# Two pairs of heads share their last 64 keys in a quartered attention, with loads one pair further ahead

## The chip, the cores and the metric

The kernel runs on one core of a Trainium2 chip. The metric is the device time of one execution in microseconds; the kernel before takes 988.81 us (median of three runs, 988.07 to 988.83). Four engines matter here: TensorE (PE in the profile) multiplies matrices into PSUM, which has eight banks; VectorE (DVE) and ScalarE (ACT) work elementwise; SyncE (SP) issues the DMAs that bring data from HBM. Each engine takes its instructions in the order in which the program gives them, and waits where one of them needs a result that is not there.

## The reference

Three stages, all in float32, on 1792 tokens (4 batches of 448) and 768 features:

```
# attention: 4 batches, 12 heads, 448 positions, 64 wide, with a sigmoid in place of the softmax
attn = sigmoid(q @ k.T / sqrt(64) - log(448));  x = attn @ v          # heads joined: 1792 x 768
# gated layer
xn = x / sqrt(mean(x*x) + 1e-6) * g;  x2 = (silu(xn @ w_gate) * (xn @ w_val)) @ w_out   # 768 -> 1536 -> 768
# experts: each token to the one of 8 with the largest logit
e = argmax(x2 @ gate);  out = p_e * (relu(x2 @ w1[e]) @ w2[e])                          # 768 -> 1024 -> 768
```

The weights of the gated layer reach the kernel as 64-bit numbers, 128 x 768 at a time, and have to be made into 32-bit ones on the chip.

## The kernel before

The work goes batch by batch. `attention(b)` makes the 768 x 448 block of one batch; `moe1(b)` is the gated layer on it; the experts come after all four batches. The program is written out by hand in the order in which each engine is to take it: generators yield after each small step, and a driver takes steps of several of them in turn. Attention of batch b+1 is taken in steps between the pieces (nine matmuls each) of `moe1(b)`.

Batches 0 and 1 use `in_quarters`. It takes the heads in six pairs, and the 448 keys of a pair in four steps: three of 128 keys, and a last one of 64. A matmul there is 64 x 64 x 448 in float32, done in two passes (two instructions), and uses a quarter of the 128 x 128 array: which half of the rows it uses follows from the half of the partitions from which it reads, which half of the columns from the half into which it writes. `quarters(t)` makes the scores of a step: with 128 keys that is four quarters (two heads, two blocks of 64 keys), which fill the array. With the last 64 keys there are two, on one diagonal: head 0 on the upper rows and left columns, head 1 on the lower rows and right columns. `weights(t)` is ScalarE's sigmoid out of PSUM, one instruction for each bank: two in a full step, one in the last. `weighted(t)` multiplies by the values, again four quarters or two, and adds up in two banks, `sums`, one for each half of the rows:

```
sums[p][i][h], v4[o, c, x, :], a[x if c < NC - 1 else 0][o],       # L686
```

After the last step of a pair `both` (L693) adds the two banks: ScalarE copies one into `xt` (L695), VectorE adds the other (L696). Two steps later ScalarE squares the result (L600, L603), and VectorE adds the squares up (L604), for the root mean square. Weighted sums lag behind the scores by two steps in batch 0, by one in batch 1.

The scores of a step wait for PSUM banks: even steps use two `sc` banks, odd steps two `mm` banks, which the gated layer uses later.

Loads. `load_pair` (L503) brings q and k of a pair, `load_v` (L514) its values; the pair goes into one of two buffers (`RQK = 2`). At the first step of a pair the next pair is loaded, into the buffer that the pair before has just left; at its third step, the next pair's values. All of it is issued by SP, in the order of the program, between the loads of 64-bit weights, `load_64` (L203).

Conversion of the weights. `narrow` (L211) takes one 128 x 768 block of 64-bit words: three instructions of VectorE (L219, L223, L227), and then the load of the block three further on. There are 36 blocks. While attention of batch 0 runs, the driver takes one and two of these instructions in turn at the steps 2 to 21, which is 30 of them, 10 blocks:

```
for _ in range(1 + n % 2 if 2 <= n < 22 else 0):                  # L1198
    next(conv)
```

In `moe1(0)` five go with each unit of 36 matmuls (`operations_due`); `ahead` (L282) takes more where the next unit's block would be missing. `split_w` (L243) then makes of each block a high part (ScalarE, L250) and a low part (VectorE, L253) for the three matmuls of `three` (L297 to L299). The first two of these splits stand at the steps 20 and 22 of attention of batch 0.

The pace of attention of batch 1 inside `moe1(0)` is `attention_due` (L53): 26 steps, spread over 55 pieces. Six of its steps have been taken before, while batch 0's last sums go through the root mean square (L773 to L817).

Of the kernel before, what the change touches and what calls it, by code (L numbers as in the profile page):

```python
# [9 lines left out]
F32 = mybir.dt.float32  # L10
F32R = mybir.dt.float32r
# [8 lines left out]
B, H, S, D = 4, 12, 448, 64  # L20
# [9 lines left out]
NC = S // CT  # L30
# [16 lines left out]
RQK = 2  # L47

KW = S + 64


def attention_due(b, n):

    main = H // 2 * NC + 2 if b == 0 else H * NC + 5
    if n < 55:
        return main * (n + 1) / 55
    return main + n - 54
# [39 lines left out]
def f32(ap):  # L97
    return ap.bitcast(F32)
# [3 lines left out]
def block_kernel(ctx, tc, qkp, qk, v, wg, wv, wo, g, gate, w1, w2, consts, out):  # L102
    nc = tc.nc
# [13 lines left out]
    s_a, aq = opened("aq", side="right", reuse_waits="tile")  # L117
# [15 lines left out]
    start = cpool.tile([128, 1], F32, name="start")  # L133
# [111 lines left out]
    def split_w(n, i):  # L245
        w = w32.pop(2 * n + i)
        h = wp.tile([128, KD, 128], F32R, tag="wh", name="wh", bufs=3)
        l = wp.tile([128, KD, 128], F32R, tag="wl", name="wl", bufs=3)
        w3 = w.rearrange("p (c k) -> p c k", k=128)
        nc.scalar.copy(out=h, in_=w3)  # L250

        def low():
            nc.vector.tensor_tensor(out=l, in0=w3, in1=f32(h), op=ALU.subtract)  # L253
            split_done[0] += 1
            if NU <= n + 1 < NU * B:
                load_32(n + 1, i)

        later(1, low)
        spl[n, i] = (h, l)
# [243 lines left out]

    def load_pair(b, p):

        r = aq.tile([128, S + KW], F32, tag="rqk", name="rqk", bufs=RQK)
        nc.sync.dma_start(out=r[:, : 2 * S], in_=qkp[b, p])
        raw_a[b, "pair", p] = r

    raw_v = {}  # L510
# [1 line left out]
    gated = []  # L512

    def load_v(b, p):  # L514
        rv = aq.tile([128, 4 * 128], F32, tag="rv", name="rv", bufs=2)
# [24 lines left out]
    def attention(b):  # L540
# [89 lines left out]
        def in_quarters():  # L630

            sums, score, weight = {}, {}, {}
            mm = [m[:, :S] for m in spare]
            n = H // 2 * NC
            halves = [slice(0, D), slice(D, 2 * D)]

            def quarters(t):
                p, c = divmod(t, NC)  # L640
                r = raw_a[b, "pair", p]

                if c % 2 and not gated:
                    banks = mm[: 1 + (c < NC - 1)]
                else:
                    banks = [sc_bank([128, S], "psc") for x in range(1 + (c < NC - 1))]
                for x, h in enumerate(halves):
                    for i, o in enumerate(halves):
                        if c < NC - 1:
                            k = S + 128 * c + D * i  # L650
                            to = banks[x][o]
                        elif i == x:
                            k = S + 128 * c
                            to = banks[0][o]
                        else:
                            continue
                        nc.tensor.matmul(to, r[h, k : k + D], r[h, :S], start=True, stop=True)  # L657
                score[t] = banks

            def weights(t):  # L660
                act = dict(func=AF.Sigmoid, bias=logs, scale=1.0 / math.sqrt(D))
                weight[t] = []
                for i, p in enumerate(score.pop(t)):
                    if t % NC == NC - 1:
                        a = f32(aq.tile([128, S], F32R, tag="al", name="aj", bufs=3))
                    elif i == 0:
                        a = aq.tile([128, S], F32, tag="a", name="a", bufs=4)
                    else:
                        a = f32(aq.tile([128, S], F32R, tag="ah", name="a2", bufs=4))
                    nc.scalar.activation(out=a, in_=p, **act)  # L670
                    weight[t].append(a)

            def weighted(t):
                p, c = divmod(t, NC)
                if c == 0:
                    if b == 0 and p % 2:
                        sums[p] = [mm[2], mi_bank([128, S], "pav")]
                    else:
                        sums[p] = [av_bank([128, S], "pav") for i in range(2)]
                a = weight.pop(t)  # L680
                v4 = raw_v[b, p].rearrange("s (c j d) -> s c j d", j=2, d=D)
                for x, h in enumerate(halves):
                    for i, o in enumerate(halves):
                        if c == NC - 1 and i != x:
                            continue
                        nc.tensor.matmul(  # L686
                            sums[p][i][h], v4[o, c, x, :], a[x if c < NC - 1 else 0][o],
                            start=(c == 0), stop=(c == (NC - 1 if i == x else NC - 2)),
                        )
                if c == NC - 1:  # L690
# [12 lines left out]
            fresh()  # L703
            coming = iter(())
            lag = 2 - b
            for t in range(n + lag):
                p, c = divmod(t, NC)
                if t < n:
                    if c == 0 and p > 0:
                        load_next(p + 1)  # L710
                    if c == 2:
                        load_v(*((b, p + 1) if p + 1 < H // 2 else (b + 1, 0)))
                    quarters(t)
                if t == n:
                    load_next(H // 2 + 1)
                    if b == 1:
                        coming = prep(2, 0)
                if t >= lag:
                    weighted(t - lag)
                step()  # L720
                if t < n:
                    weights(t)
                next(coming, None)
                yield
            for _ in coming:
                pass

        def load_next(p):
            if p < H // 2:
                load_pair(b, p)  # L730
            elif b == 0:
                load_pair(1, p - H // 2)
            else:
                load_qk(2, p - H // 2)
# [447 lines left out]


    att = {b: attention(b) for b in range(B)}
    for n in range(H // 2 * NC + 2):
# [12 lines left out]
        for _ in range(1 + n % 2 if 2 <= n < 22 else 0):  # L1198
            next(conv)
        tick()  # L1200
        if n in (20, 22):
            split_w(0, n // 2 - 10)
    ahead_of = 0
    for _ in att[0]:
        tick()
# [202 lines left out]
```

## Time and profile before

| | |
|---|---|
| runs (us) | 988.83, 988.81, 988.07; median 988.81 |
| profiled execution | 988.29 us, of it 986.2 us from the first to the last instruction |
| granted TensorE clock, mean | 0.998 of full speed |
| busy, share of the span | PE 98%, PEld (weight loads) 84%, DVE 65%, ACT 47%, POOL 2% |
| chain that ended last | PE 85%, DVE 6%, DMA 4%, ACT 1% |
| quartered matmuls in it | L657 (scores) and L686 (values), batches 0 and 1 |

In the profile a step of quartered attention shows as rows of L657 and L686. A matmul's own time there is long, as it holds the way through the array; what one costs is read from the distance between starts. The first attention lies from 4 to 45 us, the root mean square after it up to 58 us, the gated layer of batch 0 with attention of batch 1 between its pieces from 58 to 247 us.

### The profile page before, as it was taken

The numbers are of one execution on the slowest core, as the hardware profiler recorded it, in microseconds if no ns is written. First come the engines' busy times: TensorE is split into PE (matmuls) and PEld (weight loads), VectorE is DVE, ScalarE is ACT, GpSimd is POOL, SyncE is SP. The second block draws the span as 40 slices with busy tenths as digits, with TensorE's granted clock in tenths as the row PEclk, the third lists the DMA queues.
The fourth block names the chain that finished last, engine by engine and source line by source line (L and its number), as shares of the span: only waits on it lengthen the run. The fifth ranks groups of instructions, "written<-read, shape, count | busy, mean of one in ns | idle before, by whom it ended". The sixth has DMA issues, their size and how long they took to land.

```text
span 986.2 us, 14474 instructions
## 1 busy us (share of the span) xinstructions
PE 963.8 (98%) x5334; PEld 829.0 (84%) x5334; DVE 637.2 (65%) x1103; ACT 463.6 (47%) x776; POOL 14.9 (2%) x43
## 2 busy tenths in 40 slices
PE   8989999989999999999999999999999999999996
PEld 3467766777999999899999988999889988889996
DVE  5778866787798774779877465654446744444454
ACT  6743443424788872578877233332322232232230
POOL 0000000020000001000000100000000000000000
PEclk9999999999999999999999999999999999999999
DMA  8949653677544435644342569433577659838632
GB/s 323 341 166 350 243 192 119 211 244 228 184 123 138 154 101 165 195 167 126 124 144 80 143 219 319 129 99 129 142 220 235 199 172 370 296 113 289 170 65 52
DMA packets 121457, 184.33 MB, mean 187 GB/s; under 512 B 62538, under 2 KB 79690, under 8 KB 121377
## 3 DMA queue, kind: packets, MB, share of 16 engines
q1 hardware_dynamic: 119344, 182.55, 57.3%
q8 instruction: 44, 0.72, 0.3%
q0 software_dynamic: 144, 0.53, 0.2%
q10 hardware_dynamic: 1888, 0.23, 0.2%
q14 instruction: 37, 0.30, 0.1%
HBM read 145.26 MB, written 37.88 MB: 186 GB/s over the span
## 4 chain that ended last, share of the span: by engine, by line
PE 85%; DVE 6%; DMA 4%; ACT 1%; issue 1%; SPq 1%; POOL 1%; DVEq 0%; ACTq 0%
PE mm L297 19%; PE mm L298 19%; PE mm L299 19%; PE sc L297 4%; PE sc L298 4%; PE sc L299 4%; PE pav L584 2%; PE psc L551 2%; PE psc L657 2%; PE psc L552 2%; PE pav L686 2%; PE pav L586 1%; DMA xd<-x2s 1%; DVE wl L253 1%; DVE xl L808 1%
## 5 line engine op out<-in xcount | busy, mean ns | idle before, releaser
L297 PE MATMUL mm<-xh,wh 128*128 128x448 f32 x576 | 213.5, 371 | 1.3 <-ACT xh L817 1.0
L298 PE MATMUL mm<-xl,wh 128*128 128x448 f32 x576 | 210.8, 366 | 0.2 <-DVE xl L808 0.2
L299 PE MATMUL mm<-xh,wl 128*128 128x448 f32 x576 | 210.1, 365 | 0.0
L253 DVE TENSOR_TENSOR wl<-w,wh 128x768 fp32r<-128x768 f32 x126 | 119.5, 948 | 30.8 <-ACT wh L250 26.4
L250 ACT CAST wh<-w 128x768 fp32r<-128x768 f32 x126 | 105.5, 838 | 52.7 <-PE mm L298 23.2
L297 PEld LDWEIGHTS mm<-xh,wh 128*128 128x128 f32 x576 | 108.2, 188 | 24.5 <-issue 9.6
L298 PEld LDWEIGHTS mm<-xl,wh 128*128 128x128 f32 x576 | 108.2, 188 | 8.8 <-DVE xl L808 0.5
L299 PEld LDWEIGHTS mm<-xh,wl 128*128 128x128 f32 x576 | 108.2, 188 | 8.7
L297 PE MATMUL mm<-hs,wh 128*128 128x448 f32 x288 | 106.3, 369 | 0.3 <-DVE xr L344 0.3
L299 PE MATMUL mm<-hs,wl 128*128 128x448 f32 x288 | 105.4, 366 | 0.1
L298 PE MATMUL mm<-hs,wh 128*128 128x448 f32 x288 | 105.5, 366 | 0.0
L297 PE MATMUL sc<-hh,w2h 128*128 128x448 f32 (+1 forms) x200 | 72.0, 360 | 0.5 <-DVE yt L910 0.5
L298 PE MATMUL sc<-hl,w2h 128*128 128x448 f32 (+1 forms) x200 | 71.2, 356 | 0.0
L299 PE MATMUL sc<-hh,w2l 128*128 128x448 f32 (+1 forms) x200 | 71.2, 356 | 0.0
L297 PE MATMUL mm<-xd,w1h 128*128 128x448 f32 x192 | 70.8, 369 | 0.0
L298 PE MATMUL mm<-xd,w1h 128*128 128x448 f32 x192 | 70.1, 365 | 0.0
L299 PE MATMUL mm<-xd,w1l 128*128 128x448 f32 x192 | 70.1, 365 | 0.0
L561 ACT ACTIVATE a<-psc,logs 128x448 f32<-128x448 f32 x96 | 61.4, 640 | 15.7 <-PE psc L552 12.0
L891 ACT ACTIVATE hh<-mm 128x448 fp32r<-128x448 f32 x32 | 17.4, 544 | 105.2 <-PE mm L299 105.2
L563 ACT ACTIVATE ah<-psc,logs 128x448 fp32r<-128x448 f32 x96 | 60.9, 635 | 0.0
L297 PEld LDWEIGHTS mm<-hs,wh 128*128 128x128 f32 x288 | 54.1, 188 | 7.9 <-issue 1.9
L299 PEld LDWEIGHTS mm<-hs,wl 128*128 128x128 f32 x288 | 54.1, 188 | 5.2 <-DVE wl L253 0.5
(214 smaller groups left out, 1569.3 us busy)
## 6 DMA issues: line engine op xcount, KB each, us to landing
w<-w32d SPq DMA_DIRECT2D x108, 384.0 KB, 4.1
w1r<-in_w SPq DMA_DIRECT2D x24, 512.0 KB, 7.2
w2r<-in_w SPq DMA_DIRECT2D x32, 384.0 KB, 6.5
rqk<-in_qk SPq DMA_DIRECT2D x24, 480.0 KB, 3.7
x2s<-x2s SPq DMA_DIRECT2D x48, 224.0 KB, 2.0
xd<-x2s SPq DMA_DIRECT2D x8, 1344.0 KB, 11.7
w<-in_wg SPq DMA_DIRECT2D x12, 768.0 KB, 6.6
w<-in_wv SPq DMA_DIRECT2D x12, 768.0 KB, 6.6
```

The costliest lines, as they stand in the source:

```text
L250: nc.scalar.copy(out=h, in_=w3)
L253: nc.vector.tensor_tensor(out=l, in0=w3, in1=f32(h), op=ALU.subtract)
L297: nc.tensor.matmul(p, wh, xh, start=(n == 0), stop=False)
L298: nc.tensor.matmul(p, wh, xl, start=False, stop=False)
L299: nc.tensor.matmul(p, wl, xh, start=False, stop=last)
L551: nc.tensor.matmul(psc, kh[:, keys], q2, start=True, stop=False)
L552: nc.tensor.matmul(psc, kl[:, keys], q2, start=False, stop=True)
L561: nc.scalar.activation(out=a, in_=psc, bias=logs, **act)
L563: nc.scalar.activation(out=ah, in_=psc, bias=logs, **act)
L584: nc.tensor.matmul(pav[h], v2[:, c, :], ah, start=(c == 0), stop=(c == 3))
L657: nc.tensor.matmul(to, r[h, k : k + D], r[h, :S], start=True, stop=True)
L686: nc.tensor.matmul(sums[p][i][h], v4[o, c, x, :], a[x if c < NC - 1 else 0][o], start=(c == 0), stop=(c == (NC - 1 if i == x else NC - 2)),)
```

## The change

The last 64 keys of two pairs of heads are put into one step. The second pair of the two uses the other diagonal: its head 1 lower rows and left columns, its head 0 upper rows and right columns. Two pairs take 4 + 3 steps, in the order (p, 0) (p, 1) (p, 2) (p, 3 with p+1's) (p+1, 0) (p+1, 1) (p+1, 2); a batch takes `QS` = 21 steps and not 24. So that the last 64 keys add to one bank alone, the sums are now kept by diagonal and not by half of the rows. The second pair's last 64 keys come first in its sums, in the `mi` bank.

As both pairs are needed by the fourth step, odd pairs have buffers of their own (of the tags `qkh` and `v2`, which batches 2 and 3 use later), the pair after next is loaded at the first step of a pair, and so are the next pair's values.

The conversions go with the steps 2 to 17 and not 2 to 21: 24 instructions, 8 blocks. The first splits stand at the steps 18 and 20. The pace of attention of batch 1 is 23 steps over 55 pieces.

```diff
-    main = H // 2 * NC + 2 if b == 0 else H * NC + 5
+    main = QS + 2 if b == 0 else H * NC + 5          # QS = H // 2 * (NC - 1) + H // 4
...
+            order = []
+            for p in range(0, H // 2, 2):
+                order += [(p, c) for c in range(NC)] + [(p + 1, c) for c in range(last)]
...
-                        if c < NC - 1:
-                            k = S + 128 * c + D * i
-                            to = banks[x][o]
-                        elif i == x:
+                        if c < last:
+                            to, r, head = banks[x], raw_a[b, "pair", p], h
+                            k = S + 128 * c + D * i
+                        else:
+
+                            to, r, head = banks[x], raw_a[b, "pair", p + x], halves[x ^ i]
                             k = S + 128 * c
-                            to = banks[0][o]
-                        else:
-                            continue
-                        nc.tensor.matmul(to, r[h, k : k + D], r[h, :S], start=True, stop=True)
+                        nc.tensor.matmul(to[o], r[head, k : k + D], r[head, :S], start=True, stop=True)
...
+            def add_up(p, c, x, i, a):
+
+                v4 = raw_v[b, p].rearrange("s (c j d) -> s c j d", j=2, d=D)
+                y = p % 2
+                k = x ^ i ^ y
+                first, end = (0, last if k == 0 else last - 1) if y == 0 else (last if k == 0 else 0, last - 1)
+                nc.tensor.matmul(
+                    sums[p][k][halves[x]], v4[halves[i], c, x, :], a[halves[i]], start=(c == first), stop=(c == end)
+                )
...
+                if c == 0 and p % 2 == 0:
+                    sums[p] = [av_bank([128, S], "pav") for i in range(2)]
+                elif c == 0:
+                    sums[p].append(mm[2] if b == 0 else av_bank([128, S], "pav"))
+                if c == last:
+                    sums[p + 1] = [mi_bank([128, S], "pav")]
...
-                    if c == 0 and p > 0:
-                        load_next(p + 1)
-                    if c == 2:
+                    if c == 0:
                         load_v(*((b, p + 1) if p + 1 < H // 2 else (b + 1, 0)))
+                        load_next(p + 2)
...
-        for _ in range(1 + n % 2 if 2 <= n < 22 else 0):
+        for _ in range(1 + n % 2 if 2 <= n < 18 else 0):
             next(conv)
         tick()
-        if n in (20, 22):
-            split_w(0, n // 2 - 10)
+        if n in (18, 20):
+            split_w(0, n // 2 - 9)
```

On PE, from the fourth step's scores to the end of that step's values. Before (`mm_123`, `mm_124`: score banks; `a`, `aj`: weights; `rqk`, `rv`: one pair's q and k, and its values):

```order
L657 MATMUL mm_123<-rqk 64x448 x2
L686 MATMUL pav<-a,rv 64x448 x2
L686 MATMUL pav<-a_157,rv 64x448 x2
L657 MATMUL psc<-rqk 64x448 x4
L686 MATMUL pav<-a,rv 64x448 x2
L686 MATMUL pav<-a_177,rv 64x448 x2
L657 MATMUL mm_123<-rqk 64x448 x2
L657 MATMUL mm_124<-rqk 64x448 x2
L686 MATMUL pav<-aj,rv 64x448 x2
```

Now (`rqk_130`, `rv_139`: the second pair):

```order
L667 MATMUL mm_123<-rqk 64x448 x2
L667 MATMUL mm_124<-rqk_130 64x448 x2
L687 MATMUL pav<-a,rv 64x448 x2
L687 MATMUL pav<-a_161,rv 64x448 x2
L667 MATMUL psc<-rqk_130 64x448 x4
L687 MATMUL pav<-a,rv 64x448 x2
L687 MATMUL pav<-a_179,rv 64x448 x2
L667 MATMUL mm_123<-rqk_130 64x448 x2
L667 MATMUL mm_124<-rqk_130 64x448 x2
L687 MATMUL pav<-a,rv 64x448 x2
L687 MATMUL pav<-a_195,rv_139 64x448 x2
```

The fourth step has gone from two quarters to four, with two pairs in it, both for the scores and for the values; the step of two quarters that stood in each pair is gone.

On SP, from the first load up to that of the sixth block of 64-bit weights. Before (`w`: a block of 64-bit weights):

```order
L507 DMA rqk<-in_qkp 128x896
L516 DMA rv<-in_v 128x512
L507 DMA rqk<-in_qkp 128x896
L207 DMA w_149<-in_wg 128x1536
L207 DMA w_159<-in_wv 128x1536
L516 DMA rv<-in_v 128x512
L207 DMA w_179<-in_wg 128x1536
L507 DMA rqk<-in_qkp 128x896
L207 DMA w_211<-in_wv 128x1536
L516 DMA rv<-in_v 128x512
L207 DMA w_246<-in_wg 128x1536
L507 DMA rqk<-in_qkp 128x896
```

Now:

```order
L512 DMA rqk<-in_qkp 128x896
L524 DMA rv<-in_v 128x512
L512 DMA rqk_130<-in_qkp 128x896
L524 DMA rv_139<-in_v 128x512
L512 DMA rqk<-in_qkp 128x896
L209 DMA w_153<-in_wg 128x1536
L209 DMA w_163<-in_wv 128x1536
L209 DMA w_181<-in_wg 128x1536
L524 DMA rv<-in_v 128x512
L512 DMA rqk_201<-in_qkp 128x896
L209 DMA w_219<-in_wv 128x1536
L209 DMA w_254<-in_wg 128x1536
```

Each block of weights stands behind one pair more than before, and some behind one more block of values. At the seventh block, the one that the prediction speaks of, it is five pairs and four blocks of values, before it was four and four.

On DVE, in attention of batch 0, from the seventh block's conversion to the add of the fourth pair. Before (`w_316` is the seventh block, `w_349` the eighth):

```order
L219 TENSOR_SCALAR w32h<-w_316 128x768
L1195 TENSOR_TENSOR gate_83<-gate_sb,gate_83 128x6x8
L223 SCALAR_TENSOR_TENSOR w32h<-w_316,w32h 128x768
L227 SCALAR_TENSOR_TENSOR w32h<-w_316,w32h 128x768
L604 TENSOR_TENSOR ss<-ss,sq 128x448
L219 TENSOR_SCALAR w32h<-w_349 128x768
L223 SCALAR_TENSOR_TENSOR w32h<-w_349,w32h 128x768
L227 SCALAR_TENSOR_TENSOR w32h<-w_349,w32h 128x768
L696 TENSOR_TENSOR xt<-pav,xt 128x448
```

Now (`w_332` is the seventh block):

```order
L221 TENSOR_SCALAR w32h<-w_332 128x768
L612 TENSOR_TENSOR ss<-ss,sq 128x448
L1208 TENSOR_TENSOR gate_83<-gate_sb,gate_83 128x6x8
L225 SCALAR_TENSOR_TENSOR w32h<-w_332,w32h 128x768
L229 SCALAR_TENSOR_TENSOR w32h<-w_332,w32h 128x768
L712 TENSOR_TENSOR xt<-mm_125,xt 128x448
```

The add of the fourth pair stands behind seven blocks and not behind eight.

## Rows read from the trace of the kernel before

**Rows 1.** The page: busy time of the engines, share of the span, instructions.

```profile
PE 963.8 (98%) x5334; PEld 829.0 (84%) x5334; DVE 637.2 (65%) x1103; ACT 463.6 (47%) x776; POOL 14.9 (2%) x43
```

**Rows 2.** Stretches: busy us of PE, PEld, DVE, ACT, POOL; PE clock, DMA share, GB/s.

```profile
20.00:30.00 10.00, 9.61 (x92) 4.54 (x84) 8.55 (x12) 8.19 (x16) 0.00 (x0) 1.00 0.97 362
...
140.00:180.00 40.00, 39.28 (x226) 26.52 (x225) 22.43 (x31) 17.36 (x31) 0.00 (x0) 1.00 0.50 167
```

**Rows 3.** Timeline of PE, first attention: start, duration, line, tiles, count.

```profile
9.87 0.54 PE L657 MATMUL mm<-rqk 64*64 64x448 f32 x1
...
9.89 0.91 PE L657 MATMUL mm<-rqk 64*64 64x448 f32 x3
...
11.06 0.86 PE L657 MATMUL psc<-rqk 64*64 64x448 f32 x4
11.44 0.54 PE L686 MATMUL pav<-a,rv 64*64 64x448 f32 x2
...
13.63 0.54 PE L686 MATMUL pav<-aj,rv 64*64 64x448 f32 x1
...
19.64 0.54 PE L686 MATMUL mm<-aj,rv 64*64 64x448 f32 x1
```

**Rows 4.** Timeline of PE, attention of batch 1 between pieces of the gated layer.

```profile
107.33 0.98 PE L657 MATMUL psc<-rqk 64*64 64x448 f32 x8
...
112.84 0.59 PE L657 MATMUL psc<-rqk 64*64 64x448 f32 x2
...
118.33 0.98 PE L657 MATMUL psc<-rqk 64*64 64x448 f32 x8
...
120.30 0.37 PE L298 MATMUL mm<-xl,wh 128*128 128x448 f32 x1
...
123.55 0.36 PE L299 MATMUL mm<-xh,wl 128*128 128x448 f32 x1
123.84 0.98 PE L657 MATMUL psc<-rqk 64*64 64x448 f32 x8
```

**Rows 5.** Timeline of DVE: seventh block, fourth pair's add, ninth block, last add.

```profile
28.71 0.56 DVE L219 TENSOR_SCALAR w32h<-w 128x768 int32<-128x768 int32 x1 [0.55 <-DMA w<-in_wg]
30.39 0.21 DVE L1195 TENSOR_TENSOR gate<-gate_sb,gate 128x48 fp32r<-128x48 f32 x1 [1.11 <-ACT gate L1194]
...
35.37 0.62 DVE L696 TENSOR_TENSOR xt<-pav,xt 128x448 f32<-128x448 f32 x1
35.90 0.55 DVE L219 TENSOR_SCALAR w32h<-w 128x768 int32<-128x768 int32 x1
...
38.35 0.62 DVE L604 TENSOR_TENSOR ss<-ss,sq 128x448 f32<-128x448 f32 x1
...
45.58 0.62 DVE L696 TENSOR_TENSOR xt<-pav,xt 128x448 f32<-128x448 f32 x1 [1.32 <-ACT xt L695]
```

**Rows 6.** DMA issues: line, count, KB each, median us to landing.

```profile
rqk<-in_qkp SPq DMA_DIRECT2D x12, 448.0 KB, 5.9
```

**Rows 7.** Timeline of ACT, end of the first attention and just after.

```profile
36.02 0.58 ACT L603 ACTIVATE sq<-xt 128x448 f32<-128x448 f32 x1 [0.17 <-DVE xt L696]
...
39.81 1.16 ACT L670 ACTIVATE a<-mm,logs 128x448 f32<-128x448 f32 x2
40.85 1.17 ACT L670 ACTIVATE a<-psc,logs 128x448 f32<-128x448 f32 x2
41.88 0.86 ACT L250 CAST wh<-w32h 128x768 fp32r<-128x768 f32 x1
...
45.02 0.53 ACT L695 COPY xt<-mm 128x448 f32<-128x448 f32 x1 [1.05 <-PE pav L686]
...
53.57 0.53 ACT L695 COPY xt<-pav 128x448 f32<-128x448 f32 x1 [1.60 <-PE pav L686]
```

**Rows 8.** Timeline of PE: a wait for an add of batch 1's sums.

```profile
172.20 0.98 PE L686 MATMUL pav<-a,rv 64*64 64x448 f32 x6 [0.72 <-DVE xt L696]
```

**Rows 9.** Timeline of DVE: a low part behind the last conversion.

```profile
231.43 0.96 DVE L253 TENSOR_TENSOR wl<-w,wh 128x768 fp32r<-128x768 f32 x1 [0.98 <-ACT wh L250]
```

More of the change, by code (lines that the diff above doesn't have):

```diff
@@ L49 @@
 KW = S + 64
+QS = H // 2 * (NC - 1) + H // 4
 def attention_due(b, n):
-    main = H // 2 * NC + 2 if b == 0 else H * NC + 5
+    main = QS + 2 if b == 0 else H * NC + 5
     if n < 55:
@@ L504, in load_pair @@
     def load_pair(b, p):
-        r = aq.tile([128, S + KW], F32, tag="rqk", name="rqk", bufs=RQK)
+        if p % 2:
+            r = f32(aq.tile([128, S + KW], F32R, tag="qkh", name="rqk2", bufs=2))
+        else:
+            r = aq.tile([128, S + KW], F32, tag="rqk", name="rqk", bufs=RQK)
         nc.sync.dma_start(out=r[:, : 2 * S], in_=qkp[b, p])
@@ L514, in load_v @@
     def load_v(b, p):
-        rv = aq.tile([128, 4 * 128], F32, tag="rv", name="rv", bufs=2)
+        if b < 2 and p % 2:
+            rv = f32(aq.tile([128, 4, 128], F32R, tag="v2", name="rv2", bufs=3)).rearrange("s c k -> s (c k)")
+        else:
+            rv = aq.tile([128, 4 * 128], F32, tag="rv", name="rv", bufs=2)
         nc.sync.dma_start(out=rv, in_=v[b, p])
@@ L635, in in_quarters @@
             mm = [m[:, :S] for m in spare]
-            n = H // 2 * NC
             halves = [slice(0, D), slice(D, 2 * D)]
+            last = NC - 1
+            order = []
+            for p in range(0, H // 2, 2):
+                order += [(p, c) for c in range(NC)] + [(p + 1, c) for c in range(last)]
             def quarters(t):
[L640 to L644, printed above, removed]
+                p, c = order[t]
+                if t % 2 and not gated:
+                    banks = mm[:2]
                 else:
-                    banks = [sc_bank([128, S], "psc") for x in range(1 + (c < NC - 1))]
+                    banks = [sc_bank([128, S], "psc") for x in range(2)]
                 for x, h in enumerate(halves):
                     for i, o in enumerate(halves):
-                        if c < NC - 1:
+                        if c < last:
+                            to, r, head = banks[x], raw_a[b, "pair", p], h
                             k = S + 128 * c + D * i
-                            to = banks[x][o]
-                        elif i == x:
+                        else:
+                            to, r, head = banks[x], raw_a[b, "pair", p + x], halves[x ^ i]
                             k = S + 128 * c
-                            to = banks[0][o]
-                        else:
-                            continue
-                        nc.tensor.matmul(to, r[h, k : k + D], r[h, :S], start=True, stop=True)
+                        nc.tensor.matmul(to[o], r[head, k : k + D], r[head, :S], start=True, stop=True)
                 score[t] = banks
@@ L663, in weights @@
                 for i, p in enumerate(score.pop(t)):
[L664 to L666 removed]
+                    if i == 0:
                         a = aq.tile([128, S], F32, tag="a", name="a", bufs=4)
@@ L671, in weights @@
                     weight[t].append(a)
-            def weighted(t):
[L674 to L679, printed above, removed]
-                a = weight.pop(t)
[L681 to L690, printed above, removed]
+            def add_up(p, c, x, i, a):
[6 more added lines that the diff above has]
+                )
+            def weighted(t):
+                p, c = order[t]
+                a = weight.pop(t)
+                if c == 0 and p % 2 == 0:
[4 more added lines that the diff above has]
+                    sums[p + 1] = [mi_bank([128, S], "pav")]
+                for x in range(2):
+                    for i in range(2):
+                        if c < last:
+                            add_up(p, c, x, i, a[x])
+                        else:
+                            add_up(p + x, c, x ^ i, i, a[x])
+                if c == last - p % 2:
                     then(1, both, p)
@@ L705, in in_quarters @@
             lag = 2 - b
-            for t in range(n + lag):
-                p, c = divmod(t, NC)
-                if t < n:
-                    if c == 0 and p > 0:
-                        load_next(p + 1)
-                    if c == 2:
+            for t in range(QS + lag):
+                if t < QS:
+                    p, c = order[t]
+                    if c == 0:
                         load_v(*((b, p + 1) if p + 1 < H // 2 else (b + 1, 0)))
+                        load_next(p + 2)
                     quarters(t)
[L714 to L717, printed above, removed]
+                if t == QS and b == 1:
+                    coming = prep(2, 0)
                 if t >= lag:
@@ L720, in in_quarters @@
                 step()
-                if t < n:
+                if t < QS:
                     weights(t)
@@ L1184, in block_kernel @@
     att = {b: attention(b) for b in range(B)}
-    for n in range(H // 2 * NC + 2):
+    for n in range(QS + 2):
         next(att[0])
```

## The prediction

> **What bounds the kernel now.** I read the page first: PE is busy 98% of the span and no other engine over 65% [rows 1]. So time goes only where PE gets less to do, or where it waits. Next, PE's timeline in both places with quartered attention.
>
> In the first attention two quarters of scores that go on different diagonals of the array start with two of the values, all at 9.87 to 9.89 us, and four quarters then start every 11.44 - 11.06 = 0.38 us [rows 3]. I call that a slot: up to four instructions, one in each quarter. A full step has 8 instructions of scores and 8 of values, so four slots; the step with 64 keys has half of that and could do with two. But from one pair's last values (13.63) to the next one's (19.64) it is 6.01 us [rows 3], which is 16 slots: four for each of the four steps. The half step costs as much as a full one.
>
> In the gated layer of batch 0 the same shows more plainly. Steps start at 107.33, 112.84, 118.33 and 123.84 [rows 4]: the first is full, the second has half of the scores, the third half of the values, and each takes 5.5 us with its 18 matmuls of the layer. Those matmuls cost (123.55 - 120.30) / 16 = 0.203 us apart [rows 4], 18 of them 3.66, so a step costs 5.50 - 3.66 = 1.84 us, whichever it is.
>
> Last, what stands beside PE. While the first attention runs, the DMA engines are busy 97% at 362 GB/s, VectorE 86% (20 to 30 us [rows 2]): the loads of weights and their conversion keep pace with PE there by a small margin. At 140 to 180 us VectorE is busy 22.4 of 40 us and DMA half [rows 2].
>
> **The change part by part.** *Attention of batch 1.* 24 steps become 21 and the first six still lie before the layer, so three steps less stand between its pieces: 3 x 1.84 = 5.52 us. The step that trails at the end has values in four quarters and no longer in two, one slot more: +0.37. Net -5.15 us. That the shared step costs no more than a full one I take from the full steps in rows 4: the four quarters of a step are four different blocks of weights, and in its values four different streams; the shared step has nothing that these lack.
>
> *Attention of batch 0, PE's count.* Three steps less, 12 slots: 12 x 0.376 (6.01 / 16) = -4.5 us, if nothing else is late.
>
> *Batch 0, what is late.* The seventh block of weights lands at 28.7, where VectorE waits for it [rows 5]. In the new order of loads one pair more stands ahead of it, 448 KB [rows 6], at 362 GB/s [rows 2] 1.3 us: 30.0. Behind it VectorE has the block's three instructions, 38.35 - 35.90 = 2.45, a square's add and the gate's small one, 0.6 and 0.2 [rows 5], then the fourth pair's add: at 33.25, before it was 35.37 [rows 5], as it stood behind one block more. So it comes 2.1 us sooner, while PE would have it 4.5 sooner. ScalarE, whose square of this pair waited already (0.17 at 36.02 [rows 7]), waits longer, and the sigmoids behind it too, then PE for their results.
>
> From that add to the last one (45.58) it is 10.2 us before [rows 5]. Afterwards the add (0.6), a square (0.5), four steps of two sigmoids at 40.85 - 39.81 = 1.04, two splits at 0.85, two copies and a square at 0.5 follow each other [rows 7]: 8.5 us. The count of sigmoids is that of before (eight), but the wait of 1.05 for PE ahead of the last copy [rows 7] goes: the second split and a square, which stood ahead of the last sigmoid, now stand behind it and fill that time. So the last add is at 33.25 + 8.5 = 41.7: -3.9 us. Its bounds: PE's own count with the wait at the end gone, -4.5 - 1.05 = -5.5, and, with DMA pacing all, a shift of the add alone with nothing won behind it, -2.1; if the loads ahead delay by twice what I take, -0.8. I take -3.9.
>
> *The root mean square after it* is a chain of short work in which steps of batch 1 fill gaps. Step four has one sigmoid more (0.5 us), which ScalarE's idle 1.60 ahead of 53.57 [rows 7] covers; without that cover it costs 0.5. I take 0.
>
> *Loads further ahead* give PE nothing, as no wait for a pair shows in rows 3; their price is the one above. SP waits less for buffers.
>
> *Six conversions moved* (two blocks, 4.9 us of VectorE) into the gated layer of batch 0. VectorE has 17.6 us idle at 140 to 180 [rows 2], which covers most of it. Two of them end up just ahead of the last low part: before, one instruction lies between the lows there, and VectorE is idle 0.98 us as it waits for ScalarE's split [rows 9]. Two more are two thirds of a block, some 1.5 us of its 2.45, so 0.5 us shows: +0.5. Bounds 0 and 2.4 (the whole block exposed).
>
> *Waits for banks.* A pair's sums wait for the add of the pair before: 0.72 us once in batch 1 [rows 8]. Odd pairs now begin in the `mi` bank and need the other only after ScalarE's copy, so three of the five chances for this wait go; I take 0, bounds -0.7 and +1.4.
>
> *Sum.* -3.9 - 5.15 + 0.5 = -8.55 on the profiled execution of 988.29 us: 979.7. The median of the runs, 988.81, lies 0.5 above it, so 980.3.
>
> **Rules that speak against it.** The row: a full step's eight scores take 0.98 us from the first start to the last end [rows 4], where one alone lasts 0.54 [rows 3]. That is two slots (0.38 + 0.54 = 0.92) and not four (1.68), so two quarters in the same half of the rows do run together. The Trainium skill ("TensorE: Matmul & The Clock Gate", Part 3, The mechanism) has a weight load overlap a running matmul only where their row groups differ. By this, the second pair's quarters, which use the first pair's rows, would have to follow; the trace does not agree. It is the third rival.
>
> The second row: the two scores at 9.87 and 9.89 [rows 3] are a half step's, one in the upper rows, the other in the lower, and both write one bank. The Trainium skill ("TensorEngine Tiling (Array Packing)", Gotcha 1: PSUM Pressure) says that different row tiles cannot access the same bank at the same time. By this, the new sums, kept by diagonal, would make values take turns in every step; the trace does not agree, in the one place where it shows such a pair. It is the fourth rival.
>
> **The rivals.** (1) DMA paces the first attention and what PE saves there is lost to waiting: for it, 97% [rows 2] and a load that VectorE waits for [rows 5]; against it, two blocks less are loaded there. Only -0.8 of the -3.9 is left: 988.8 - 0.8 - 5.15 + 0.5 = 983.4.
>
> (2) The conversions are short at the end of the first gated layer: two blocks of which the last is exposed twice, 2 x 2.4 in place of 0.5: 980.3 + 4.3 = 984.6. For it, the low part there already waits for a split that waits for a conversion [rows 9]; against it, VectorE's idle time further ahead [rows 2].
>
> (3) The change doesn't do what it says: the second pair's quarters run behind the first one's, as half steps do. Six shared steps have four slots more, 24 x 0.376 = 9.0, which is the gain: 989.3, no change. Against it the rows above.
>
> (4) Slower: values of different row halves into one bank take turns. Place: `add_up` in each of 42 steps; price: two slots more in each, 0.75 us, 31.6 in all, so 980.3 + 31.6 = 1011.9. It decides from 12 such steps on (12 x 0.75 = 9.0). Against it, the pair of scores at 9.87; for it, that no row shows four at once.
>
> **How the numbers follow.** Forecast 0.63, rival 1 0.15, rival 2 0.10, rival 3 0.06, rival 4 0.06. A measurement of this kernel tells a change from none at about 0.2%, 2 us. Faster takes the first three, 0.88; same is rival 3, 0.06; slower rival 4, 0.06. Time 980.3. The forecast's own range, with the bounds of batch 0 (-5.5 and -2.1), of the end (+0 to +1.5) and the banks, is 977.8 to 983.0; rivals 1 and 2 reach to 983.4 and 984.6. I give 977.5 to 984.6, which leaves out rivals 3 and 4 and some of the tails.
>
> **What would show it.** Right: PE's two-pair period in the first attention 28 slots (10.5 us) where nothing waits, the shared step's four quarters starting together; the seventh block landing near 30 us and the fourth pair's add near 33.3; the first matmul of the gated layer about 3.9 us sooner; there, steps at 1.84 us, 16 and not 19. The distance from the first gated matmul to batch 1's about 4.7 us shorter. Wrong: the shared step lasting over 1.84 us; the last add of batch 0 later than 44.8; new waits of PE for VectorE near the end of the first gated layer over 2 us; any difference behind it, where nothing is changed.

## The result, and the profile after

The changed kernel takes **979.43 us** (median; 979.25 to 980.24) beside 988.82 for the kernel before on the same chip: 0.9909 of it, 95% interval 0.9894 to 0.9924. Forecast were 980.3 us, range 977.5 to 984.6. The profiled execution took 979.25 us with a span of 977.4, that is 9.0 us less than the one of before. The total fits; some of its terms don't, and their errors nearly cancel. Among the experiments, one of the five executions of the kernel with conversions as before took 2298.74 us; the median given there is of the other four.

The page first: busy time and instructions per engine, to set beside [rows 1].

```profile
PE 957.3 (98%) x5334; PEld 831.5 (85%) x5334; DVE 635.9 (65%) x1103; ACT 463.6 (47%) x776; POOL 14.4 (1%) x43
```

The same 5334 matmuls are issued as before. Nothing was taken out; instructions that ran two abreast now run four abreast. PE's timeline in the first attention of the changed kernel (columns as in [rows 3]) shows it:

```profile
7.24 0.95 PE L667 MATMUL psc<-rqk 64*64 64x448 f32 x8
...
8.75 0.94 PE L667 MATMUL mm<-rqk 64*64 64x448 f32 x8
9.50 0.94 PE L687 MATMUL pav<-a,rv 64*64 64x448 f32 x8
...
12.51 0.94 PE L687 MATMUL pav<-a,rv 64*64 64x448 f32 x8
```

The row at 8.75 has the shared step's scores, the row at 12.51 its values. Each is one row of eight, 0.94 us long, and the next row starts 0.75 later: two slots, like any full step. The same in batch 1, between the pieces of the gated layer:

```profile
101.91 0.98 PE L667 MATMUL psc<-rqk 64*64 64x448 f32 x8
...
107.42 0.98 PE L667 MATMUL psc<-rqk 64*64 64x448 f32 x8
...
177.43 0.98 PE L687 MATMUL pav<-a,rv 64*64 64x448 f32 x8
```

A step is again 5.51 us with 18 matmuls of the layer, so 1.84 by itself, as in [rows 4]; 15 of them start in the layer and not 18. The third and the fourth rival, in which quarters would take turns, are refuted by these rows.

Where the 9.0 us are, by marks on PE's timeline:

| stretch | before | after | difference |
|---|---|---|---|
| start to the first matmul of the gated layer | 58.51 | 54.61 | -3.90 |
| from there to the first logits that wait for x2 | 168.28 | 161.36 | -6.92 |
| from there to batch 1's first gated matmul | 10.39 | 11.91 | +1.52 |
| from there to the end of the span | 749.03 | 749.48 | +0.45 |
| outside the span | 2.09 | 1.85 | -0.24 |

The prediction named any difference behind the changed part as a sign of being wrong, and there is one of 0.45. The kernel before, run again, has 749.63 in that stretch, so two executions of one program differ by as much.

The fourth pair's add is at 33.23 where 33.25 was forecast, but not for the reason given. DVE's timeline in the changed kernel, to set beside [rows 5]:

```profile
27.95 0.57 DVE L221 TENSOR_SCALAR w32h<-w 128x768 int32<-128x768 int32 x1
...
31.24 0.21 DVE L1208 TENSOR_TENSOR gate<-gate_sb,gate 128x48 fp32r<-128x48 f32 x1 [2.19 <-ACT gate L1207]
...
33.23 0.61 DVE L712 TENSOR_TENSOR xt<-mm,xt 128x448 f32<-128x448 f32 x1
...
42.17 0.62 DVE L712 TENSOR_TENSOR xt<-mm,xt 128x448 f32<-128x448 f32 x1
```

and ACT's, beside [rows 7]:

```profile
29.50 0.53 ACT L711 COPY xt<-pav 128x448 f32<-128x448 f32 x1 [0.76 <-PE mm L687]
29.93 1.16 ACT L678 ACTIVATE a<-mm,logs 128x448 f32<-128x448 f32 x2
30.97 0.24 ACT L1207 CAST gate<-gate_sb 128x48 fp32r<-128x48 f32 x1
...
33.94 0.58 ACT L611 ACTIVATE sq<-xt 128x448 f32<-128x448 f32 x1 [1.66 <-DVE xt L712]
```

The seventh block has landed when VectorE wants it: 27.95, no wait. Behind it VectorE stands still for 2.19 us, for the small split of the gate, whose ScalarE half (30.97) is queued behind a copy that waited 0.76 us for PE, and two sigmoids. VectorE is now early and the order of its queue makes it wait; the add, and behind it ScalarE (1.66) and PE (0.72 at 35.09), wait with it.

In this execution the DMA engines moved more than before, with more of it issued ahead. Two stretches before, with the columns of [rows 2] (the last is GB/s):

```profile
12.00:20.00 8.00, 8.00 (x76) 3.98 (x74) 6.41 (x10) 5.95 (x11) 0.00 (x0) 1.00 0.96 336
20.00:28.00 8.00, 8.00 (x79) 4.04 (x74) 7.83 (x11) 6.19 (x12) 0.00 (x0) 1.00 0.97 362
```

and the same two after:

```profile
12.00:20.00 8.00, 8.00 (x83) 3.57 (x76) 7.55 (x11) 6.31 (x13) 0.00 (x0) 1.00 0.99 376
20.00:28.00 8.00, 8.00 (x88) 6.49 (x87) 7.90 (x12) 7.13 (x14) 0.00 (x0) 1.00 1.02 399
```

(40 + 37) GB/s over 8 us each are 0.62 MB more than before, above the 448 KB that stand ahead of the block.

Not every execution has this. The kernel with conversions sooner in the layer (below) has the same first attention, and there the two stretches show 369 and 346 GB/s, and VectorE waits for the block. The gate's split still makes it wait longest ahead of the add, as DVE's timeline of that kernel shows:

```profile
29.51 0.56 DVE L221 TENSOR_SCALAR w32h<-w 128x768 int32<-128x768 int32 x1 [0.52 <-DMA w<-in_wg]
...
32.33 0.21 DVE L1208 TENSOR_TENSOR gate<-gate_sb,gate 128x48 fp32r<-128x48 f32 x1 [1.73 <-ACT gate L1207]
...
34.32 0.62 DVE L712 TENSOR_TENSOR xt<-mm,xt 128x448 f32<-128x448 f32 x1
```

Over 12 to 28 us the eleven traces with loads further ahead have 354 to 391 GB/s, the two of the kernel before 348 and 349. That the loads ahead raise the rate fits this; no run has them changed by themselves in the changed kernel.

The +1.52 is at the end of the layer. PE's timeline there, after:

```profile
215.97 0.38 PE L385 MATMUL mm<-x2s,gate 128*16 128x448 f32 x1 [0.67 <-ACT x2s L340]
217.42 0.37 PE L385 MATMUL mm<-x2s,gate 128*16 128x448 f32 x1 [1.07 <-DVE x2s L343]
218.07 0.44 PE L299 MATMUL mm<-hs,wh 128*128 128x448 f32 x1 [0.28 <-DVE xr L346]
...
219.71 0.57 PE L300 MATMUL mm<-hs,wh 128*128 128x448 f32 x1
220.08 0.57 PE L301 MATMUL mm<-hs,wl 128*128 128x448 f32 x1
```

and before:

```profile
226.79 0.37 PE L383 MATMUL mm<-x2s,gate 128*16 128x448 f32 x1 [0.55 <-ACT x2s L338]
228.24 0.38 PE L383 MATMUL mm<-x2s,gate 128*16 128x448 f32 x1 [1.07 <-DVE x2s L341]
228.89 0.44 PE L297 MATMUL mm<-hs,wh 128*128 128x448 f32 x1 [0.27 <-DVE xr L344]
...
230.15 0.37 PE L298 MATMUL mm<-hs,wh 128*128 128x448 f32 x1
230.36 0.37 PE L299 MATMUL mm<-hs,wl 128*128 128x448 f32 x1
```

The waits are the same within 0.12 us. Behind them matmuls start 0.21 us apart before, 0.37 after. What differs is in the column third from the end, the granted clock. The stretch after: half (1.2 GHz), and 9 matmuls in 3 us.

```profile
219.00:222.00 3.00, 3.00 (x9) 2.65 (x10) 2.15 (x3) 0.67 (x1) 0.00 (x0) 0.50 1.08 327
```

The one that answers to it before: full (2.4 GHz), and 16.

```profile
230.00:233.00 3.00, 3.00 (x16) 2.73 (x15) 1.95 (x3) 2.00 (x3) 0.00 (x0) 1.00 0.87 187
```

### The profile page after: what moved, and what is told of

It reads as the page before. It is cut to its first block, busy times and chain, and to the rows that moved or that the text cites. A ratio compares the mean times of both kernels' runs of the same rounds, so it can differ in the third digit from the quotient of the medians.

```text
span 977.4 us, 14479 instructions
## 1 busy us (share of the span) xinstructions
PE 957.3 (98%) x5334; PEld 831.5 (85%) x5334; DVE 635.9 (65%) x1103; ACT 463.6 (47%) x776; POOL 14.4 (1%) x43
## 4 chain that ended last, share of the span: by engine, by line
PE 92%; DVE 4%; DMA 1%; issue 1%; ACT 1%; SPq 0%; DVEq 0%; ACTq 0%
PE mm L299 21%; PE mm L301 20%; PE mm L300 20%; PE sc L299 4%; PE sc L300 4%; PE sc L301 4%; PE pav L687 3%; PE psc L667 3%; PE psc L559 2%; PE pav L592 2%; PE psc L560 2%; PE pav L594 2%; PE mm L667 1%; PE sc L1068 1%; PE mm L385 1%
```

## The experiments

Times are medians, with the ratio to the kernel before and its 95% interval. All but one start from the changed kernel.

**Each batch alone.** `SHARED` names the batches whose half steps are shared; loads are the new ones in both, conversions and splits stand where each batch 0 had them.

```diff
-                order += [(p, c) for c in range(NC)] + [(p + 1, c) for c in range(last)]
+                order += [(p, c) for c in range(NC)] + [(p + 1, c) for c in range(last if b in SHARED else NC)]
```

> Steps are shared in batch 1 alone; batch 0 takes 24 steps as before, with its 30 conversion instructions, but keeps the loads one pair further ahead. Theory (the front gains by PE's twelve slots, the layer by three steps of 1.84 us and a wait of 0.9 that goes): first gated matmul at 58.5 us as before, from there to batch 1's first gated matmul about 6.9 us less than before, or 5.4 if the half clock comes behind the gap near its end; 981.9 to 983.4 us. Rival (the loads ahead bring the front's gain): first gated matmul at 55 to 56, 978.5 to 980 us.

> Steps are shared in batch 0 alone; batch 1 takes 24 steps. Theory: first gated matmul at 54.6 as in the changed kernel, the distance to batch 1's first gated matmul as before (plus 1.5 if the half clock comes); 984.9 to 986.4 us. Rival (the two conversions moved into the layer cost time there when the layer has no steps to lose): the distance 2 to 5 us longer than before, 987 to 990 us.

Batch 1 alone: 981.19 us, 0.9925 (0.9912 to 0.9939). This is 0.7 under its forecast. The layer is 6.92 us shorter (first gated matmul to batch 1's), and begins at 58.21, almost as before; that settles the term of batch 1, and that loads issued further ahead do not by themselves shorten the start. Its end of the layer, on PE:

```profile
219.59 0.38 PE L390 MATMUL mm<-x2s,gate 128*16 128x448 f32 x1 [0.57 <-ACT x2s L345]
221.03 0.37 PE L390 MATMUL mm<-x2s,gate 128*16 128x448 f32 x1 [1.07 <-DVE x2s L348]
221.68 0.44 PE L304 MATMUL mm<-hs,wh 128*128 128x448 f32 x1 [0.27 <-DVE xr L351]
...
222.94 0.37 PE L305 MATMUL mm<-hs,wh 128*128 128x448 f32 x1
```

The same waits, and full clock behind them. Batch 0 alone: 984.35, 0.9956 (0.9942 to 0.997), 0.6 under its forecast; the layer then begins at 55.80, and behind its waits for x2 the half clock shows. To batch 1's first gated matmul it is 179.16 us, 178.67 before, so not the 2 to 5 more of its rival. The two gains, 7.4 and 4.2 us, are 2.2 more than both together have (9.4). By their mean clocks (0.997 or 0.998) all executions of batch 1 alone and four of five of batch 0 alone are without the stretch of half clock that the changed kernel's profile shows; that would be 1.5 of the 2.2. It is not shown, and the intervals leave room for the rest.

**The gate's split.** It is moved from step 15 of the first attention into the gated layer, whose logits are the first to need it.

```diff
-        if n == 15:
-            nc.scalar.copy(out=gate_2[:, :, :E], in_=gate_sb)
-            nc.vector.tensor_tensor(
-                out=gate_2[:, :, E:], in0=gate_sb, in1=f32(gate_2[:, :, :E]), op=ALU.subtract
-            )
...
+                if n == 24:          # in the loop over moe1(0), the same two instructions
```

> The changed kernel, with the split of the gate weights (one instruction of ScalarE, one of VectorE) moved out of the first attention into the gated layer. Theory (VectorE's fourth add came at 33.2 because the gate's part on VectorE waited 2.2 us for ScalarE's, not because of the seventh block, which had landed at 27.8): fourth add near 31, PE's wait of 0.7 at 35 gone, first gated matmul 1.0 to 1.3 earlier, 978.2 us. Rival (loads pace the first attention, as the prediction had it): VectorE waits for the eighth block instead, first gated matmul as it is, 979.4 us.

977.34 us, 0.989 (0.9874 to 0.9905). VectorE's adds on its timeline:

```profile
31.39 0.62 DVE L712 TENSOR_TENSOR xt<-mm,xt 128x448 f32<-128x448 f32 x1
...
40.98 0.62 DVE L712 TENSOR_TENSOR xt<-mm,xt 128x448 f32<-128x448 f32 x1
```

The fourth add comes 1.84 us sooner though nothing about the loads was touched: the gate held it, not the seventh block. The first gated matmul comes at 53.43 and not 54.61, 1.2 us sooner, as forecast. The medians are 2.1 apart, but their intervals overlap.

**Conversions as before.** 30 of them in the first attention again, splits at the steps 20 and 22.

```diff
-        for _ in range(1 + n % 2 if 2 <= n < 18 else 0):
+        for _ in range(1 + n % 2 if 2 <= n < 22 else 0):
```

> The changed kernel with the conversions left where they were before: 30 instructions at the steps 2 to 21, first splits at 20 and 22. Theory (two blocks more do not fit beside 21 steps; DMA and VectorE then end last): first gated matmul 2 to 3 us later than in the changed kernel; at the end of the layer one conversion instruction between the last low parts, not three, and no stretch at half clock there (-1.5): 980 to 981 us. Rival (VectorE and DMA have room): first gated matmul at 54.6 to 55, 978 us.

980.9 us (four executions, 979.2 to 981.64), 0.9916 (0.9901 to 0.9931). In the profiled one the layer begins at 57.30 and not 54.61; its length is 173.28 us, with 173.27 in the changed kernel. So the six conversions cost the layer nothing. Of the 2.7 us at the start, 1.1 is the clock (below): beside the next kernel, whose clock rose as late and whose layer begins at 55.70, their place in the first attention is worth 1.6. The medians are 1.5 apart, with intervals that overlap. That the half clock would go was a miss: it stays.

**Conversions sooner in the layer.**

```diff
-    return 2 if n % 4 == 3 else 1
+    return 2 if n % 4 == 3 or 24 <= n < 60 and n % 4 == 1 else 1
```

> The changed kernel, but VectorE takes two conversion instructions and not one at some more places of the first gated layer, so that the 64-bit weights are converted well before its end. Theory (the last 1.6 us that the change should have brought are lost where PE, behind its waits of 1.04, 1.44 and 0.65 us at 216 to 218 us, runs 3.41 us at half its clock, and the first of these waits has to do with the conversions that stand in VectorE's way): the first wait shrinks by up to 1 us, and with less waiting the half clock may go too; 979.4 - 0.5 - 1.6 = 977.3, with no stretch of half clock, first gated matmul to batch 1's about 171.2 us. Rival (these waits are a chain of ScalarE's and VectorE's splits of x2 which no conversion lengthens): the waits stay at 1.04, 1.44, 0.65, the half clock too, 979.4, distance 173.3 us.

> The gate's split in the first gated layer (as in e3_gate_later) and the earlier conversions together. If both act apart: 977.3 - 2.1 = 975.2, first gated matmul at 53.4 us and no half clock. If the waits at the end of the layer are no matter of the conversions: like e3_gate_later, 977.3.

Alone 979.04, 0.9898 (0.9881 to 0.9915): no better than the changed kernel. With the gate's split moved 975.95, 0.9873 (0.9857 to 0.989). In both the waits for x2 are gone: in the second, PE starts 17 and 16 matmuls in the two stretches where it stood in the changed kernel.

```profile
213.00:216.00 3.00, 3.00 (x17) 2.68 (x16) 2.90 (x6) 2.25 (x4) 0.00 (x0) 1.00 0.40 145
216.00:219.00 3.00, 3.00 (x16) 2.69 (x15) 1.35 (x2) 1.27 (x2) 0.00 (x0) 1.00 0.88 170
```

So conversions did stand in VectorE's way there. But they now stand in its way earlier: in both kernels PE waits 2.15 us for the sum of squares, 0.62 in the changed kernel. In the first one the half clock comes behind the wait after that, 2.58 us for the row sums at 206.20; in the second behind this wait, for 6.8 us in place of 3.4, as PE's timeline there shows:

```profile
192.02 1.26 PE L786 MATMUL pm<-ones,ss 128*112 128x1 f32 x8 [2.15 <-DVE ss L612]
...
193.67 0.57 PE L300 MATMUL mm<-hs,wh 128*128 128x448 f32 x1
```

**Logits one unit later**, so that PE need not wait for x2 at all (batch 0 alone).

```diff
-                    if oc > 0:
-                        logits(b, oc - 1)
+                    if oc > (b == 0):
+                        logits(b, oc - 1 - (b == 0))
```

> The changed kernel with batch 0's logits issued on PE one unit (36 matmuls) later, so that they need not wait for the halves of x2; nothing moves on VectorE or ScalarE. Theory (the half clock follows from PE standing still there, in waits of 1.04, 1.44 and 0.65 us): the waits go, 2.5 us beyond the ordinary distance of 0.2 us, and the 3.41 us at half clock with them, 1.5 us; as PE's next units may then wait in turn for the bank that x2 is read from, some 1 us of this comes back: 979.4 - 3.0 = 976.4. Rival A (the half clock has its place here whatever PE does): the waits go, the half clock stays, 977.9. Rival B (PE only meets the wait elsewhere, since the next unit needs the bank that VectorE reads x2 from): same sum of waits, 979.4.

> The gate's split in the first gated layer and the logits one unit later, together. Theory: both act apart, 977.3 - 3.0 = 974.3 with no half clock; with rival A 975.8; with rival B 977.3.

> As e8_gate_and_logits_later, and seven conversion instructions taken sooner in the first half of the first gated layer, where in e6 nine were taken later on and made PE wait 2.5 us for the sum of squares of batch 1. Theory: that wait does not grow (under 1 us), the wait for the row sums (1.6 us in the changed kernel) does not either, and with the conversions out of the way at the layer's end it is 973 to 974.5. Rival (VectorE has no room left in the first half either): the sum of squares comes late again, by over 2 us, and it is not faster than e8.

979.5, 0.9908 (0.9891 to 0.9924); 978.74, 0.9898 (0.9881 to 0.9914); 978.23, 0.9902 (0.9885 to 0.9918). Rival B holds, as the first one's rows show:

```profile
215.07 0.56 PE L385 MATMUL mm<-x2s,gate 128*16 128x448 f32 x2
218.02 0.44 PE L299 MATMUL mm<-hs,wh 128*128 128x448 f32 x1 [2.38 <-DVE xr L346]
...
220.20 0.58 PE L300 MATMUL mm<-hs,wh 128*128 128x448 f32 x1
```

The logits no longer wait, and the next unit waits 2.38 us for its bank, which VectorE has not read yet. My reading of three waits for x2 as three costs was wrong: 0.67, 1.07 and 0.28 there (2.0 together) and 2.38 here read as one lateness of VectorE, which PE meets where it first needs anything of it. The half clock stays too. The third kernel's conversions did not lengthen the wait for the sum of squares to over 2 us (1.3), but did not bring 973 to 974.5 either: its next unit waits 2.11 us, for a split of ScalarE.

**The kernel before, unchanged**, to see whose the half clock is.

> The kernel before, with nothing changed, to see what of the half clock belongs to the change. If the half clock is a matter of the execution: the ratio is 1.000 within 0.2%, and executions with a mean clock of 0.995 to 0.996 appear here too, about as often as those of 0.998; if the profiled one is of these, its trace shows a stretch of half clock behind a wait of PE. If it is the change's: all executions have 0.998.

988.42 us, 0.9994 (0.9984 to 1.0003). The mean granted clock of its executions was 0.998 in seven, 0.997 in two, 0.996 in three. Over all 52 executions of this kernel in and beside the experiments it was 0.998 in 22 (median 988.18 us), 0.997 in 8, and 0.996 or less in 22 (988.87). In the traces at hand 0.998 goes with no such stretch (before, this one, batch 1 alone), 0.995 or 0.996 with one of 3.4 us, 0.994 with one of 6.8; the mean also counts the last 3.6 to 5.8 us of the span, at half clock in every trace. So by its mean clock the kernel before has the stretch too, in some two of five executions. No trace shows it there, as both of its profiled executions have 0.998.

That does not clear the change. A mean clock of 0.996 or less is found in three of the four executions of the changed kernel and in 29 of 37 of it and its variants that share in both batches, but in one of ten where only one batch shares. Whether the change makes the stretch more frequent is open.

**Gate and conversions, first half of the layer.**

```diff
-    return 2 if n % 4 == 3 else 1
+    return 2 if n % 4 == 3 or 16 <= n < 44 and n % 4 == 1 else 1
```

> The gate's split in the first gated layer (as in e3_gate_later) and seven conversion instructions sooner in the first half of that layer (as in e9), with the logits where they were. Theory (what stands in the way at the layer's end is VectorE's work that was put off): the waits for x2 shrink by over 1 us against e3 and the sum of squares stays under 1.5 us late, 976.0 (like e6). Rival (conversions taken sooner only wait for loads): like e3, 977.3.

977.05, 0.988 (0.9865 to 0.9896): not told apart from the gate's move alone. The sum of squares stayed under 1.5 us late, but the waits for x2 came back, divided otherwise. PE's timeline at the sum of squares:

```profile
192.12 0.92 PE L786 MATMUL pm<-ones,ss 128*112 128x1 f32 x8 [1.15 <-DVE ss L612]
...
193.96 0.58 PE L300 MATMUL mm<-hs,wh 128*128 128x448 f32 x1
```

and later on the same timeline:

```profile
216.33 0.38 PE L385 MATMUL mm<-x2s,gate 128*16 128x448 f32 x1 [1.07 <-ACT x2s L340]
...
218.01 0.37 PE L300 MATMUL mm<-hs,wh 128*128 128x448 f32 x1
```

Here the half clock follows the wait of 1.15 and not the later one of 1.07. Of the kernels run, the gate's split moved with conversions at 24 to 59 has the lowest median, 975.95, 3.5 us under the changed kernel; their intervals (to 0.989, and from 0.9894) do not meet.

## Why the prediction was right, step by step

The range held and faster came out. By the terms of the sum:

| step | forecast | measured |
|---|---|---|
| batch 1, three steps less | -5.52 | -5.5, inside the -6.92 |
| its trailing step | +0.37 | 0 |
| waits for banks | 0 (bounds -0.7, +1.4) | -0.7 |
| batch 0 and its tail | -3.9 (-5.5 to -2.1) | -3.9 in this execution, -2.8 at the clock of before |
| end of the layer, conversions | +0.5 | 0; the half clock +1.5 in this execution |

**Right.** A shared step costs what a full one costs, in scores and in values. That is the mechanism on which all the gain rests. The Trainium skill ("TensorE: Matmul & The Clock Gate", Part 3, The mechanism) has a weight load overlap a running matmul only where their row groups differ, and ("TensorEngine Tiling (Array Packing)", Gotcha 1: PSUM Pressure) says that different row tiles cannot access the same bank at the same time. From each the prediction worked out a rival in which quarters take turns; eight instructions in 0.94 us, scores and values, do not bear either out.

**The trailing step** failed in its reading: I priced it at one slot more because its values go from two quarters to four. Before, that half step already took two slots; the table of marks has no place for the +0.37, and 177.43 in the changed kernel costs what 188.02 did before:

```profile
188.02 0.97 PE L686 MATMUL pav<-aj,rv 64*64 64x448 f32 x4
```

Four instructions in 0.97 us, as eight in 0.98. The prediction itself had said that a half step costs as much as a full one; the term contradicts it.

**Waits for banks.** The 0.72 of [rows 8] is gone; I took 0 and had -0.7 as the bound. Three steps and this wait make 6.2 of the 6.92. The other 0.7 is not accounted for; a shorter wait for the sum of squares (0.62, before 0.85) does not explain it, as batch 1 alone has 0.90 there and shortens by as much.

**Batch 0: right number, wrong road.** The step "the seventh block lands at 30.0" failed: in the profiled execution it landed before 27.95, at 376 and 399 GB/s where I had divided by 362. In the kernel with conversions sooner it came at about 29.5, near my number, and did not set the add either. What sets the add in both is the gate's split, which [rows 5] showed with a wait of 1.11, and which I carried along as 0.2 us of work, without its wait. From that add to the last one it is 8.94 us (33.23 to 42.17) and not 8.5; from there to the first gated matmul 12.44, before 12.93, where I took no difference.

What made the total come out was the clock. In the first microseconds slots are 0.75 us apart, twice the later distance, up to a moment that differs between executions. I read that as half clock. The clock column cannot show it: it has 1.00 there, as the trace's records of the clock only begin where full clock is granted, at 9.45 us before, 7.24 in the changed kernel and 9.74 in the one with conversions sooner. In each that is where the rows become shorter. PE's timeline from its first matmul on, before:

```profile
4.25 1.77 PE L657 MATMUL psc<-rqk 64*64 64x448 f32 x8 [4.25 <-DMA rqk<-in_qkp]
...
7.29 1.73 PE L657 MATMUL psc<-rqk 64*64 64x448 f32 x8
8.79 1.26 PE L686 MATMUL pav<-a,rv 64*64 64x448 f32 x8
```

and in the kernel with conversions sooner, whose first attention is that of the changed one:

```profile
4.25 1.77 PE L667 MATMUL psc<-rqk 64*64 64x448 f32 x8 [4.25 <-DMA rqk<-in_qkp]
...
7.29 1.74 PE L667 MATMUL psc<-rqk 64*64 64x448 f32 x8
8.79 1.41 PE L687 MATMUL pav<-a,rv 64*64 64x448 f32 x8
...
55.70 0.47 PE L299 MATMUL mm<-xh,wh 128*128 128x448 f32 x1 [1.01 <-ACT xh L830]
```

In the changed kernel's own profile the row at 7.24 is already 0.95 long: three slots less at half clock, 3 x 0.37 = 1.1 us. With the clock as late as before (to 0.15 us), the same code begins the layer at 55.70 (batch 0 alone: 55.80), so its gain is 58.51 - 55.70 = 2.8 us: inside my bounds, and 1.1 short of my value.

**The end of the layer.** The +0.5 for two exposed conversions is not there: with them moved back the layer is as long (173.28 and 173.27). What showed in its place, +1.5, is the stretch of half clock, which the kernel before, by its mean clock, has in some of its executions. I had no term for it, nor for a difference between executions at all.

With the clock alike in both profiles, at the start and at the layer's end, the difference would be about 9.0 - 1.1 + 1.5 = 9.4 us, as an estimate. The two nearly offset each other, so that the total came this close is in part luck, and it proves little about the terms. The forecast's own range was added up wrongly: its bounds give 977.5 to 984.5, not 977.8 to 983.0; the range stated holds both.

Rival 1 (DMA paces the start) and rival 2 (conversions short at the layer's end) did not come. Rival 1 left 0.8 us of gain in the first attention, and batch 0 alone gains 4.2: the gate's split ends last ahead of the add, also where the load came late. Against rival 2 stand the 173.28 and 173.27.

**Open:** what decides in an execution whether PE's clock falls behind one of these waits. Waits of the same length had it (conversions as before) and did not (batch 1 alone), so their length alone does not decide; experiments with the waits moved only moved it. Open, too, is whether sharing in both batches makes it more frequent.

## What to carry to other kernels

Work that uses part of the array costs the slot, not the share: pair half steps that go to different quarters, and count slots, not instructions. When one engine is made faster, look in the other engines' queues for small instructions that stand ahead of what it needs; here two of 0.2 us held an add back, and with them moved it came 1.8 us sooner, the next layer 1.2. Compare the granted clock of two profiles before reading differences of 1 or 2 us, at the start as much as in the middle.

## What the runs showed of the hardware that was not expected

- The granted clock of TensorE went to half for 3.4 us (once 6.8) in the midst of dense work, behind waits of 1.1 to 2.6 us or during one, in ten of thirteen traces. From the first wait for x2 to batch 1's first gated matmul it is 10.37 to 10.39 us without it (before, batch 1 alone) and 11.62 to 11.91 with it (the changed kernel, batch 0 alone, the gate's split moved, conversions as before). By the mean clock, executions of one program differ in whether they have it.
- At the start, slots were 0.75 us apart for 4 slots in the profile of the changed kernel and for 7 in that of before, a difference of 1.1 us. It is none of the change's: the same code had full clock granted at 7.24 and at 9.74 us in two executions.
- With loads issued further ahead, 376 and 399 GB/s were moved in one execution where 336 and 362, at a busy share of 0.96 and 0.97, had looked like a full queue; another execution of the same code had 369 and 346.
